# Layer two's block products over pairs of 512-token blocks, and output matmuls taken from a queue

## The chip, the core and the metric

The kernel runs on one core of one Trainium2 chip. The metric is device time in microseconds (us) of one execution, the median of several runs. Engines are called PE (matmuls) with PEld (its weight loads), DVE (vector), ACT (scalar) and SP, whose queue issues every DMA of this kernel. A PE matmul here has a 128x128 stationary operand and a moving operand of 512 or 256 columns. All values are 32 bit.

## What is computed

An attention stage over pooled keys and values makes x (4608 tokens x 512). Layer one and layer two follow:

```
h = x @ w_in                         # 512 x 2048
g = h * (1 / (1 + exp(-1.702 * h)))
x = g @ w_out                        # 2048 x 512
a, b = x @ w_a, x @ w_b              # 512 x 1536 each
return ((a * b) @ w_out2)            # 1536 x 512
```

Inputs are double precision, and the kernel splits every value into a high and a low part, so each product of the reference is three matmuls: high x high, high x low, low x high.

## The kernel before

The 4608 tokens stand in 9 blocks of 512. Work goes in passes. Layer one has two passes (`passes` 0 and 1, with 6 and 10 of its 16 slices of 128 hidden columns), layer two three (passes 2 to 4, with 4 of its 12 slices `f` each). A pass goes over all 9 blocks, and in a block over its slices; one (pass, block, slice) is a step. Partial sums over slices stay in PSUM within a pass and go through DRAM between passes: pass 2 writes them (tile `ys`, L513 to L518), pass 3 reads and writes, pass 4 reads and writes the output (L520 to L524).

Layer one: 12 matmuls make `h` and 12 make `acc` in a step, all of 512 columns (`mm3`, L132 to L135).

Layer two: for one slice, a and b over the 512 tokens are a 2 x 2 block matrix (two columns of the weights by two halves of 256 tokens), and seven block products replace eight (`products`, L419). Their operands are sums of blocks of x (seven tiles `xo` a block, 512 KB each, made at the end of pass 1 by `store_operands`, L480, kept in DRAM as `yd` and loaded again in each pass) and of weights (`wc`). Product number n is six matmuls of 256 columns into one of the PSUM banks X (two buffers), Y and Z (one each), L438. Three of the products are followed by a copy by ACT (L444, L446, L448), the others by a DVE operation (L450 to L459); DVE and ACT then make `chi` and `clo`, the two parts of a * b, for each token half (`parts`, L427). A bank that is accumulated on must have been read by that copy or operation before PE goes on writing it: product 6 waits for L444, 3 for L446, 7 for L448, 4 for L454.

The output matmuls (`out_rows`, L464) take `chi` and `clo` of 128 tokens as the stationary operand and the slice's rows of w_out2 (`wo`) as moving, three matmuls of 512 columns (L470, L471, L472) for one row c of four. `mixed` (L576) runs the products of one step between the output rows of the step before, in the order of `ORDER` (L574), where P is a product and O a row:

```
ORDER = ("P1", "P5", "O2", "P6", "O3", "P3", "P2", "P7", "O0", "O1", "P4")
```

PE's order is fixed by `after_last` (L404); the other engines' orders come from a scheduler at build time, and each engine runs its instructions in that order. `finish` (L507) evicts the four sums at the end of a block. SBUF tiles come from pools: `wp` (13 buffers of 8 KB a partition: weights and raw data), `xp` (11 of 4 KB: operands), `p2` (`st` with two buffers, `part`, `raw`, `v`), `gp`, `yp` (two buffers for `ys`).

Of the kernel before, what the change touches and what calls it, by code (L numbers as in the profile page):

```python
# [9 lines left out]
F32 = mybir.dt.float32  # L10
# [14 lines left out]
def tile_kernel(ctx, tc, q, k, v, w_in, w_out, w_a, w_b, w_o2, out):  # L25
# [30 lines left out]
    HALF = N // 2  # L56

    const = ctx.enter_context(tc.tile_pool(name="const", bufs=1))
    wp = ctx.enter_context(tc.tile_pool(name="wp", bufs=13))
    xp = ctx.enter_context(tc.tile_pool(name="xp", bufs=11))  # L60
# [82 lines left out]
    yd = [dram.tile([P, 7, 2, 2, HALF], F32, name=f"yd{j}") for j in range(NB)]  # L143
# [7 lines left out]
    def x_tiles():  # L151

        return [[xp.tile([P, 2, N], F32R, tag="x", name=nm) for _ in range(2)] for nm in ("xhi", "xlo")]
# [4 lines left out]
    def load_x(i, j):  # L158
        if passes[i][0] == 1:
            x_t[i, j] = x_tiles()  # L160
            for e in range(2):
                for h in range(2):
                    nc.sync.dma_start(out=f32(x_t[i, j][e][h]), in_=xd[j][:, e, 2 * h:2 * h + 2])
            return
        x_t[i, j] = [None] * 7
        for o in USED:
            x_t[i, j][o] = xp.tile([P, 2, 2, HALF], F32R, tag="x", name="xo")
            nc.sync.dma_start(out=f32(x_t[i, j][o]), in_=yd[j][:, o])
# [250 lines left out]
    def products(i, j, f):  # L419

        banks = {nm: ps2.tile([P, HALF], F32, tag=nm, name=nm, bufs=2 if nm == "X" else 1) for nm in "XYZ"}
        X, Y, Z = (banks[nm] for nm in "XYZ")
        s = p2.tile([P, 3, HALF], F32, tag="st", name="s")
        chi, clo = (gp.tile([P, 2, HALF], F32R, tag=tag, name=nm) for tag, nm in (("ghi", "chi"), ("glo", "clo")))
        g_t[i, j, f] = (chi, clo)

        def parts(col, src):  # L427
            nc.scalar.copy(out=chi[:, col], in_=src)  # L428
            nc.vector.tensor_tensor(out=clo[:, col], in0=src, in1=f32(chi[:, col]), op=ALU.subtract)  # L429

        def product(n):
            c, o, nm = PRODUCTS[n]
            w, at_ = w2_t[f, c]
            x = x_t[i, j][o]
            for kk in range(2):
                ks = slice(kk * P, (kk + 1) * P)
                for m, (we, xe) in enumerate(((0, 0), (0, 1), (1, 0))):
# [4 lines left out]
                    ))  # L442
            if n == 1:
                nc.scalar.copy(out=s[:, 0], in_=X)  # L444
            elif n == 5:
                nc.scalar.copy(out=s[:, 1], in_=Y)  # L446
            elif n == 6:
                nc.scalar.copy(out=s[:, 2], in_=X)  # L448
            elif n == 3:
                nc.vector.tensor_tensor(out=s[:, 2], in0=s[:, 2], in1=Y, op=ALU.add)  # L450
            elif n == 2:
                nc.vector.tensor_tensor(out=s[:, 0], in0=s[:, 0], in1=Z, op=ALU.add)
            elif n == 7:
                nc.vector.tensor_tensor(out=s[:, 1], in0=s[:, 1], in1=X, op=ALU.add)  # L454
                made = nc.vector.tensor_tensor(out=s[:, 1], in0=s[:, 1], in1=s[:, 2], op=ALU.mult)  # L455
                anchors[i, j, f] = made.ins
                parts(1, s[:, 1])
            else:
                nc.vector.tensor_tensor(out=s[:, 0], in0=s[:, 0], in1=X, op=ALU.mult)  # L459
                parts(0, s[:, 0])  # L460

        return product

    def out_rows(f, cs_, oa, c, first, last):  # L464

        chi, clo = (t[:, c // 2] for t in cs_)
        w = w_t[3, f // 2]
        whi, wlo = w[:, f % 2, :], w[:, 2 + f % 2, :]
        ts = slice(c % 2 * P, (c % 2 + 1) * P)
        after_last(nc.tensor.matmul(out=oa[c], lhsT=chi[:, ts], rhs=whi, start=first, stop=False))  # L470
        after_last(nc.tensor.matmul(out=oa[c], lhsT=chi[:, ts], rhs=wlo, start=False, stop=False))  # L471
# [35 lines left out]
    def finish(i, j, sums):  # L507
# [17 lines left out]
        if i == 1:  # L525
            store_operands(j, part_t[i, j])
# [340 lines left out]
```

## Time and profile before

| | us |
|---|---|
| median of three runs (1835.01 to 1837.60) | 1836.38 |
| profiled execution, its own time | 1838.84 |
| span of its instructions | 1837.1 |
| PE busy in the span | 1777.5 |
| DVE busy | 1092.1 |
| ACT busy | 641.2 |

The profiled execution's time is its span and 1.74 us around it. It is 2.46 us (0.13%) above the median. Attention lies mixed with pass 0 up to about 450 us, pass 1 runs to about 964 us, and layer two's three passes take the rest.

How to read the rows: start and length in us from the span's start; then the engine, the line of the kernel, the operation, the tiles as out<-in, the shape and how many alike follow each other (x6). In brackets stands idle time of the engine just before, and what ended it. A PE matmul's shown length has its drain in it, so successive matmuls overlap; what one costs is the distance of starts.

### The profile page before, as it was taken

To read this page: it belongs to the slowest core of one execution; us is meant where nothing else is said; L and a number is where in the kernel's file an instruction comes from. 1 tells how busy PE (TensorE), PEld (TensorE's weight loads), DVE (VectorE), ACT (ScalarE), POOL (GpSimd) and SP (SyncE) were. 2 spreads that over 40 slices of the span, in tenths; PEclk is the share of its full clock that TensorE was granted. 3 is DMA by queue.
4 is the path that set the end of the run, shared out by engine and by line. 5 is a ranking of instruction groups with operands and counts; after the bars stand their busy time and mean duration, and the time that the engine had idled before them with its cause. 6 is when DMAs were issued, how large, how long until landed. Compare 5 with 4: busy or idle time off the path is not lost.

```text
span 1837.1 us, 27304 instructions
## 1 busy us (share of the span) xinstructions
PE 1777.5 (97%) x10536; PEld 1548.8 (84%) x10536; DVE 1092.1 (59%) x2157; ACT 641.2 (35%) x1754; POOL 1.7 (0%) x8
## 2 busy tenths in 40 slices
PE   5789999999999999999997999998999999999999
PEld 4667888888888888888886999998999999999998
DVE  6885666655986677677535665663444444444444
ACT  5645655553332333333332323332222222222222
POOL 0000000000000000000000000000000000000000
PEclk7889999999999999999998999999999999999999
DMA  8364444335545546555683656479454548464642
GB/s 296 106 204 148 145 157 154 105 98 184 195 154 184 224 177 247 212 200 186 237 293 144 252 198 250 175 279 360 173 206 161 208 160 320 157 221 149 221 158 104
DMA packets 100546, 358.31 MB, mean 195 GB/s; under 512 B 11232, under 2 KB 11232, under 8 KB 92064
## 3 DMA queue, kind: packets, MB, share of 16 engines
q1 hardware_dynamic: 100416, 356.56, 54.2%
q8 instruction: 83, 1.36, 0.3%
q14 instruction: 47, 0.39, 0.1%
HBM read 238.55 MB, written 117.96 MB: 194 GB/s over the span
## 4 chain that ended last, share of the span: by engine, by line
PE 89%; DVE 5%; DMA 4%; ACT 2%; issue 0%; ACTq 0%; DVEq 0%; SPq 0%
PE X L438 16%; PE Y L438 8%; PE h L133 7%; PE acc L133 7%; PE h L134 7%; PE acc L134 7%; PE h L135 7%; PE acc L135 7%; PE acc L470 5%; PE acc L471 5%; PE acc L472 5%; PE Z L438 4%; PE px L284 2%; DMA part<-ys 2%; PE sc L239 2%; PE pt L271 1%
## 5 line engine op out<-in xcount | busy, mean ns | idle before, releaser
L438 PE MATMUL X<-xo,wc 128*128 128x256 f32 x2592 | 364.1, 283 | 11.5 <-ACT s L444 11.0
L438 PEld LDWEIGHTS X<-xo,wc 128*128 128x128 f32 x2592 | 348.5, 191 | 31.1 <-ACT s L444 11.8
L428 ACT CAST chi<-s 128x256 fp32r<-128x256 f32 x216 | 87.9, 407 | 439.7 <-DVE s L455 346.4
L133 PE MATMUL h<-xhi,w 128*128 128x512 f32 x576 | 227.8, 396 | 0.8 <-ACT xhi L88 0.5
L134 PE MATMUL h<-xlo,w 128*128 128x512 f32 x576 | 226.3, 393 | 0.0
L135 PE MATMUL acc<-ghi,w 128*128 128x512 f32 x576 | 225.8, 392 | 0.0
L134 PE MATMUL acc<-glo,w 128*128 128x512 f32 x576 | 225.8, 392 | 0.0
L135 PE MATMUL h<-xhi,w 128*128 128x512 f32 x576 | 225.7, 392 | 0.0
L438 PE MATMUL Y<-xo,wc 128*128 128x256 f32 x1296 | 190.2, 283 | 0.0
L385 ACT ACTIVATE g<-h 128x512 f32<-128x512 f32 x144 | 86.2, 599 | 293.7 <-PE h L135 270.7
L438 PEld LDWEIGHTS Y<-xo,wc 128*128 128x128 f32 x1296 | 178.0, 191 | 9.6
L388 DVE SCALAR_TENSOR_TENSOR g<-g,h 128x512 f32<-128x512 f32 x144 | 98.4, 684 | 142.1 <-ACT g L385 142.0
L133 PE MATMUL acc<-ghi,w 128*128 128x512 f32 x576 | 180.4, 401 | 2.3 <-ACT ghi L389 2.1
L470 PE MATMUL acc<-wo,chi 128*128 128x512 f32 x432 | 172.1, 398 | 4.8 <-ACT ys L515 4.8
L471 PE MATMUL acc<-wo,chi 128*128 128x512 f32 x432 | 171.9, 398 | 0.0
L450 DVE TENSOR_TENSOR s<-s,Y 128x256 f32<-128x256 f32 x108 | 45.5, 421 | 210.1 <-PE Y L438 208.0
L472 PE MATMUL acc<-wo,clo 128*128 128x512 f32 x432 | 169.2, 392 | 0.8 <-DVE clo L429 0.8
L429 DVE TENSOR_TENSOR clo<-s,chi 128x256 fp32r<-128x256 f32 x216 | 91.3, 424 | 85.9 <-ACT chi L428 85.9
L133 PEld LDWEIGHTS h<-xhi,w 128*128 128x128 f32 x576 | 109.5, 190 | 24.8 <-ACT aT L272 0.9
L135 PEld LDWEIGHTS h<-xhi,w 128*128 128x128 f32 x576 | 109.2, 190 | 23.1
L134 PEld LDWEIGHTS h<-xlo,w 128*128 128x128 f32 x576 | 109.3, 190 | 22.8 <-DVE raw L125 0.4
L133 PEld LDWEIGHTS acc<-ghi,w 128*128 128x128 f32 x576 | 107.1, 190 | 24.0 <-ACT ghi L389 2.9
(75 smaller groups left out, 2397.9 us busy)
## 6 DMA issues: line engine op xcount, KB each, us to landing
xo<-yd SPq DMA_DIRECT2D x189, 512.0 KB
yd<-st SPq DMA_DIRECT2D x63, 512.0 KB
part<-part SPq DMA_DIRECT2D x27, 1024.0 KB
part<-ys SPq DMA_DIRECT2D x72, 256.0 KB
raw<-in_moe_w_out_dram SPq DMA_DIRECT2D x28, 512.0 KB
wd<-ws SPq DMA_DIRECT2D x12, 1024.0 KB
wc<-wd SPq DMA_DIRECT2D x12, 1024.0 KB
xd<-xhi SPq DMA_DIRECT2D x18, 512.0 KB
```

The lines of the kernel that those rows point to most:

```text
L133: nc.tensor.matmul(out=o, lhsT=whi, rhs=xhi, start=first, stop=False)
L134: nc.tensor.matmul(out=o, lhsT=whi, rhs=xlo, start=False, stop=False)
L135: nc.tensor.matmul(out=o, lhsT=wlo, rhs=xhi, start=False, stop=last)
L385: nc.scalar.activation(out=g, in_=hps, func=AF.Tanh, scale=0.5 * 1.702)
L388: made = vec(nc.vector.scalar_tensor_tensor(out=g, in0=g, scalar=1.0, in1=hps, op0=ALU.add, op1=ALU.mult))
L428: nc.scalar.copy(out=chi[:, col], in_=src)
L429: nc.vector.tensor_tensor(out=clo[:, col], in0=src, in1=f32(chi[:, col]), op=ALU.subtract)
L438: after_last(nc.tensor.matmul(out=banks[nm], lhsT=w[:, at_, we, ks], rhs=x[:, xe, kk, :], start=n in FIRST and kk == 0 and m == 0, stop=kk ...
L450: nc.vector.tensor_tensor(out=s[:, 2], in0=s[:, 2], in1=Y, op=ALU.add)
L470: after_last(nc.tensor.matmul(out=oa[c], lhsT=chi[:, ts], rhs=whi, start=first, stop=False))
L471: after_last(nc.tensor.matmul(out=oa[c], lhsT=chi[:, ts], rhs=wlo, start=False, stop=False))
L472: after_last(nc.tensor.matmul(out=oa[c], lhsT=clo[:, ts], rhs=whi, start=False, stop=last))
```

## The change

It groups the blocks in layer two into units: blocks (1,2), (3,4), (5,6), (7,8) are four pairs, block 0 stands alone. Pass 1 now goes over the blocks 1 to 8 and then 0. In a pair the "two halves of tokens" of the 2 x 2 scheme are its two blocks, so each matmul of a product has 512 columns where it had 256, and there are half as many; operands of a pair are 1 MB each. Block 0 keeps 256 columns.

Output rows are no longer bound to the next step. Each row group (three matmuls) goes into a list `groups`, and `pop(n)` inside a step's table runs the n oldest. The second token column's rows (4 in a pair, 2 in block 0) are queued after each slice; those of the first column (`held[0, f]`, tiles `hi` and `lo`, five buffers) wait in SBUF until the unit's last slice and are then queued row by row over all four slices. A sum is evicted as its last group runs (`evict`). All big SBUF tiles, operands, weights, partial sums of layer one and (in layer two) raw weights, share one pool `wp` of 19 buffers. The last block's operand stores take their staging tiles from `wp`.

```diff
-    wp = ctx.enter_context(tc.tile_pool(name="wp", bufs=13))
-    xp = ctx.enter_context(tc.tile_pool(name="xp", bufs=11))
+    units = [(j, j + 1) for j in range(1, NB, 2)] + [(0,)]
+    NU2 = len(units)
+    order = [list(range(NB)), [j for u in units for j in u]] + [list(range(NU2))] * (L2 - L1)
+    wp = ctx.enter_context(tc.tile_pool(name="wp", bufs=19))
...
+    def load_operand(i, u, n):
+        o = USED[n]
+        if len(units[u]) == 2:
+            t = wp.tile([P, 2, 2, N], F32R, tag="w", name="xo")
...
+        nc.sync.dma_start(out=f32(t), in_=yd[u][:, o])
...
+    def out_rows(i, f, col, ti, j, c, first, last):
...
+        if first:
+            accs[i, j, c] = acc.tile([P, N], F32, tag="acc", name="acc")
+        oa = accs[i, j, c]
+        after_last(nc.tensor.matmul(out=oa, lhsT=chi[:, ts], rhs=whi, start=first, stop=False))
+        after_last(nc.tensor.matmul(out=oa, lhsT=chi[:, ts], rhs=wlo, start=False, stop=False))
+        after_last(nc.tensor.matmul(out=oa, lhsT=clo[:, ts], rhs=whi, start=False, stop=last))
+        if last:
+            evict(i, j, c, accs.pop((i, j, c)))
+
+    def pop(n):
+        for g in groups[:n]:
+            g()
+        del groups[:n]
...
-    def products(i, j, f):
-        banks = {nm: ps2.tile([P, HALF], F32, tag=nm, name=nm, bufs=2 if nm == "X" else 1) for nm in "XYZ"}
+    def products(i, u, f, table):
+        n_ = N if pair else HALF
+        banks = {nm: ps2.tile([P, n_], F32, tag=nm, name=nm, bufs=2 if nm == "X" else 1) for nm in "XYZ"}
...
+        for what in table:
+            if what[0] == "P":
+                product(int(what[1]))
+            else:
+                pop(int(what[1]))
+        groups.extend(g for _, g in rows_of(1, f, held.pop((1, f))))
+        if last:
+            per_f = [list(rows_of(0, f_, held.pop((0, f_)))) for f_ in fs]
+            for ti in range(n_ // P):
+                groups.extend(p[ti][1] for p in per_f)
...
+    def evict(i, j, c, a):
+        to = part[2][j][:, c, :] if i in WRITES else out[j * N + c * P:j * N + (c + 1) * P, :]
+        if i in READS:
+            t = part_t.pop((i, j, c))
+            nc.vector.tensor_tensor(out=t, in0=a, in1=t, op=ALU.add)
+        else:
+            t = yp.tile([P, N], F32, tag="y", name="ys")
...
+        nc.sync.dma_start(out=to, in_=t)
...
+            st = p2.tile([P, 2, 2, w_], F32R, tag="st", name="st", bufs=2)
+        else:
+            st = wp.tile([P, 2, 2, w_], F32R, tag="w", name="st")
...
-    ORDER = ("P1", "P5", "O2", "P6", "O3", "P3", "P2", "P7", "O0", "O1", "P4")
+    FIRST_F = ("O2", "P1", "O2", "P5", "O2", "P6", "O2", "P3", "O2", "P2", "O1", "P7", "O3", "P4")
+    OTHER_F = ("P1", "P5", "O1", "P6", "O1", "P3", "P2", "O1", "P7", "O3", "P4")
...
+            before.setdefault((i - 1, NU2 - 1, passes[i - 1][1][0]), []).extend(loads(i))
...
+                before.setdefault((i, u, fs[2]), []).extend(operands(i, u + 1))
```

The digit after O is now a number of groups to pop. The next unit's operands are asked for from the third step of a unit, a pass's weights and first operands from the first step of block 0 in the pass before.

**PE, a step within a pass.** Before, from products 4 and 1 (which run into each other) on; L438 is a product's matmul, L470 to L472 one output row:

```order
L438 MATMUL X<-xo,wc 128x256 x12
L438 MATMUL Y<-xo,wc 128x256 x6
L470 MATMUL acc<-wo,chi 128x512
L471 MATMUL acc<-wo,chi 128x512
L472 MATMUL acc<-wo,clo 128x512
L438 MATMUL X<-xo,wc 128x256 x6
L470 MATMUL acc<-wo,chi 128x512
L471 MATMUL acc<-wo,chi 128x512
L472 MATMUL acc<-wo,clo 128x512
L438 MATMUL Y<-xo,wc 128x256 x6
L438 MATMUL Z<-xo,wc 128x256 x6
```

The same place in the changed kernel, in a pair (L492 is a product's matmul, L445 to L447 one group of the list):

```order
L492 MATMUL X<-xo,wc 128x512 x12
L492 MATMUL Y<-xo,wc 128x512 x6
L445 MATMUL acc<-wo,ghi 128x512
L446 MATMUL acc<-wo,ghi 128x512
L447 MATMUL acc<-wo,glo 128x512
L492 MATMUL X<-xo,wc 128x512 x6
L445 MATMUL acc<-wo,ghi 128x512
L446 MATMUL acc<-wo,ghi 128x512
L447 MATMUL acc<-wo,glo 128x512
L492 MATMUL Y<-xo,wc 128x512 x6
L492 MATMUL Z<-xo,wc 128x512 x6
```

The sequence is the same, the matmuls are twice as wide, and one such step now stands for two blocks.

**PE, from the last step of a pass (block 0) to the next pass.** Before, this place reads as within a pass; from product 3 of a step to product 1 of the next:

```order
L438 MATMUL Y<-xo,wc 128x256 x6
L438 MATMUL Z<-xo,wc 128x256 x6
L438 MATMUL X<-xo,wc 128x256 x6
L470 MATMUL acc<-wo,chi 128x512
L471 MATMUL acc<-wo,chi 128x512
L472 MATMUL acc<-wo,clo 128x512
L470 MATMUL acc<-wo,chi 128x512
L471 MATMUL acc<-wo,chi 128x512
L472 MATMUL acc<-wo,clo 128x512
L438 MATMUL X<-xo,wc 128x256 x12
```

Now, at the end of pass 2:

```order
L492 MATMUL Y<-xo_9578,wc 128x256 x6
L492 MATMUL Z<-xo_9581,wc 128x256 x6
L492 MATMUL X<-xo_9581,wc 128x256 x6
L492 MATMUL X<-xo_9584,wc 128x256 x6
L445 MATMUL acc<-wo,ghi 128x512
L446 MATMUL acc<-wo,ghi 128x512
L447 MATMUL acc<-wo,glo 128x512
L445 MATMUL acc<-wo,ghi 128x512
L446 MATMUL acc<-wo,ghi 128x512
L447 MATMUL acc<-wo,glo 128x512
L492 MATMUL X<-xo,wc 128x512 x6
```

The list has run empty here: products 3, 2, 7 and 4 follow each other with no group between them, and the first groups after product 4 are those of the `ghi` that product 7 has just started.

**ACT, from layer one to layer two.** `st` is the staging tile of the last block's operand stores (L88 before, L92 after). Before:

```order
L444 COPY s<-X 128x256
L446 COPY s<-Y 128x256
L88 CAST st<-part 128x512
L448 COPY s<-X 128x256
L428 CAST chi<-s 128x256
L88 CAST st<-part 128x512
L428 CAST chi<-s 128x256
L88 CAST st<-part 128x512 x5
L444 COPY s<-X 128x256
```

Now:

```order
L500 COPY s<-X 128x512
L502 COPY s<-Y 128x512
L92 CAST st<-part 128x512 x2
L504 COPY s<-X 128x512
L477 CAST ghi<-s 128x512
L92 CAST st<-part 128x512
L477 CAST hi<-s 128x512
L500 COPY s<-X 128x512
L92 CAST st<-part 128x512
L502 COPY s<-Y 128x512
```

Five stagings stood together ahead of the second step's first copy; now the seven stand singly or in pairs between the copies.

## Rows read from the trace of the kernel before

**Rows 1.** Page: engines' busy time, and PE, its granted clock in 40 slices.

```profile
PE 1777.5 (97%) x10536; PEld 1548.8 (84%) x10536; DVE 1092.1 (59%) x2157; ACT 641.2 (35%) x1754; POOL 1.7 (0%) x8
...
PE   5789999999999999999997999998999999999999
...
PEclk7889999999999999999998999999999999999999
```

**Rows 2.** Stages: PE, PEld, DVE, ACT, POOL busy (instructions), clock, DMA share, GB/s.

```profile
500.00:950.00 450.00, 450.00 (x1987) 372.61 (x1986) 308.53 (x530) 151.01 (x244) 0.00 (x0) 1.00 0.57 208
1300.00:1800.00 500.00, 500.00 (x3469) 466.93 (x3468) 228.29 (x515) 118.13 (x322) 0.00 (x0) 1.00 0.54 196
```

**Rows 3.** Timeline, PE, one step of pass 3 (from product 4 on).

```profile
1400.73 1.59 PE L438 MATMUL X<-xo,wc 128*128 128x256 f32 x12
1402.16 0.88 PE L438 MATMUL Y<-xo,wc 128*128 128x256 f32 x6
1402.88 0.40 PE L470 MATMUL acc<-wo,chi 128*128 128x512 f32 x1
...
1403.58 0.87 PE L438 MATMUL X<-xo,wc 128*128 128x256 f32 x6
...
1408.52 1.59 PE L438 MATMUL X<-xo,wc 128*128 128x256 f32 x12
```

**Rows 4.** Groups by shape: DVE and ACT on 256 and on 512 columns.

```profile
L385 ACT ACTIVATE g<-h 128x512 f32<-128x512 f32 x144 | 86.2, 599 | 293.7 <-PE h L135 270.7 <-DVE glo L393 19.4 <-DVE raw L644 3.5
...
L521 DVE SCALAR_TENSOR_TENSOR part<-acc,part 128x512 f32<-128x512 f32 x108 | 70.7, 686 | 29.8 <-PE acc L472 21.4 <-DMA xo<-yd 4.9 <-PE acc L135 3.5
...
L454 DVE TENSOR_TENSOR s<-s,X 128x256 f32<-128x256 f32 x108 | 45.5, 421 | 30.5 <-PE X L438 30.5
```

**Rows 5.** Timeline, DVE, after product 7 of the last steps.

```profile
1828.17 0.42 DVE L454 TENSOR_TENSOR s<-s,X 128x256 f32<-128x256 f32 x1 [0.30 <-PE X L438]
1828.63 0.42 DVE L455 TENSOR_TENSOR s<-s 128x256 f32<-128x256 f32 x1
1829.53 0.43 DVE L429 TENSOR_TENSOR clo<-s,chi 128x256 fp32r<-128x256 f32 x1 [0.47 <-ACT chi L428]
```

**Rows 6.** Timeline, from layer one to layer two, several engines.

```profile
981.45 0.62 ACT L88 CAST st<-part 128x512 fp32r<-128x512 f32 x1 [1.68 <-DMA yd<-st]
...
986.24 1.65 PE L438 MATMUL X<-xo,wc 128*128 128x256 f32 x6 [10.98 <-ACT s L444]
...
988.96 1.48 PE L438 MATMUL Y<-xo,wc 128*128 128x256 f32 x6
990.24 1.37 PE L438 MATMUL Z<-xo,wc 128*128 128x256 f32 x6
```

**Rows 7.** Waits of PE: what for, us in total, times, longest.

```profile
PE pt L271 <- DVE at L263: 19.2, 6, 5.6
...
PE acc L470 <- ACT ys L515: 4.8, 2, 4.1
PE acc L472 <- DVE clo L429: 0.8, 3, 0.4
```

**Rows 8.** Timeline, PE and ACT, around the end of pass 2.

```profile
1279.59 0.60 ACT L515 ACTIVATE ys<-acc 128x512 f32<-128x512 f32 x1 [2.06 <-DMA part<-ys]
...
1280.24 0.80 PE L470 MATMUL acc<-wo,chi 128*128 128x512 f32 x1 [4.07 <-ACT ys L515]
...
1282.97 2.46 PE L438 MATMUL X<-xo,wc 128*128 128x256 f32 x12
1285.26 0.88 PE L438 MATMUL Y<-xo,wc 128*128 128x256 f32 x6
```

**Rows 9.** Stages of 10 us there, columns as in rows 2.

```profile
1230.00:1240.00 10.00, 10.00 (x72) 9.40 (x71) 4.80 (x11) 3.52 (x9) 0.00 (x0) 1.00 1.01 391
...
1280.00:1290.00 10.00, 9.76 (x53) 8.93 (x54) 2.25 (x5) 1.71 (x5) 0.00 (x0) 0.76 0.20 76
```

**Rows 10.** Waits of SP's queue, 960 to 1300 us, longest first.

```profile
SPq L168 <- PE X L438: 104.2, 36, 18.0
```

More of the change, by code (lines that the diff above doesn't have):

```diff
@@ L158, in load_x, with operands @@
     def load_x(i, j):
[L159 to L168, printed above, removed]
+        x_t[i, j] = x_tiles()
+        for e in range(2):
+            for h in range(2):
+                nc.sync.dma_start(out=f32(x_t[i, j][e][h]), in_=xd[j][:, e, 2 * h:2 * h + 2])
+    def load_operand(i, u, n):
[3 more added lines that the diff above has]
+        else:
+            if n % 2 == 0:
+                x_t[i, u, "both"] = wp.tile([P, 2, 2, 2, HALF], F32R, tag="w", name="xo2")
+            t = x_t[i, u, "both"][:, n % 2]
+        x_t[i, u, o] = t
+        nc.sync.dma_start(out=f32(t), in_=yd[u][:, o])
+    def operands(i, u):
+        return [op(load_operand, i, u, n) for n in range(7)]
     at = ExitStack()
@@ L417, in tile_kernel @@
     FIRST, LAST = (1, 2, 5), (2, 3, 4)
[L419 to L429 removed]
+    groups = []
@@ new lines, in pop, with st, col_tiles, rows_of @@
+    def pop(n):
+        for g in groups[:n]:
+            g()
+        del groups[:n]
+    held = {}
+    def products(i, u, f, table):
+        fs = passes[i][1]
+        pair = len(units[u]) == 2
+        n_ = N if pair else HALF
+        first, last = f == fs[0], f == fs[-1]
+        banks = {nm: ps2.tile([P, n_], F32, tag=nm, name=nm, bufs=2 if nm == "X" else 1) for nm in "XYZ"}
+        X, Y, Z = (banks[nm] for nm in "XYZ")
+        s = {}
+        def st(n):
+            s[n] = p2.tile([P, n_], F32, tag="st", name="s", bufs=4)
+            return s[n]
+        def col_tiles(pool, bufs, *tags):
+            return tuple(pool.tile([P, n_], F32R, tag=tag, name=tag, bufs=bufs) for tag in tags)
+        def parts(col, src):
+            chi, clo = col
+            nc.scalar.copy(out=chi, in_=src)
+            nc.vector.tensor_tensor(out=clo, in0=src, in1=f32(chi), op=ALU.subtract)
+        def rows_of(col_n, f, col):
+            for ti in range(n_ // P):
+                j, c = (units[u][col_n], ti) if pair else (units[u][0], 2 * col_n + ti)
+                yield c, op(out_rows, i, f, col, ti, j, c, f == fs[0], f == fs[-1])
@@ L462, in products @@
[L462 to L471, printed above, removed]
-        after_last(nc.tensor.matmul(out=oa[c], lhsT=clo[:, ts], rhs=whi, start=False, stop=last))
@@ new lines, in products, with load_part, load_rows @@
+        groups.extend(g for _, g in rows_of(1, f, held.pop((1, f))))
+        if last:
+            per_f = [list(rows_of(0, f_, held.pop((0, f_)))) for f_ in fs]
+            for ti in range(n_ // P):
+                groups.extend(p[ti][1] for p in per_f)
+    part_t = {}
+    def load_part(j):
+        part_t[j] = wp.tile([P, KD, N], F32, tag="w", name="part")
+        nc.sync.dma_start(out=part_t[j], in_=part[1][j])
+    def load_rows(i, u, col):
+        for ti in range(4 if len(units[u]) == 2 else 2):
+            j, c = (units[u][col], ti) if len(units[u]) == 2 else (units[u][0], 2 * col + ti)
+            if col == 0 and ti < 2:
+                t = yp.tile([P, N], F32, tag="y", name="part")
+            else:
+                t = p2.tile([P, N], F32, tag="part", name="part", bufs=4)
+            part_t[i, j, c] = t
+            nc.sync.dma_start(out=t, in_=part[2][j][:, c, :])
@@ L507, in finish @@
     def finish(i, j, sums):
-        layer = passes[i][0]
-        half = 0.5 if layer == 1 else 1.0
-        for c in (2, 3, 0, 1) if layer == 2 else range(4):
+        for c in range(4):
             if i not in READS:
@@ L819, in tile_kernel @@
             second(s)
+    pop(len(groups))
 def _laid_out(name, a):
```

230 lines of the change are left out of this document (141 added, 89 removed).

## The prediction

> **What bounds the kernel now.** I read the page first. PE is busy 97% of the span, DVE 59%, ACT 35%, and in the slices PE is at 9 nearly everywhere from the fifth on, with PEclk at 9 [rows 1]. So the time is a stream of matmuls plus the few places where the stream breaks, and a change is worth what it does to the distance between matmul starts, and to the breaks. Both have to be read from stages.
>
> The stages come next [rows 2]. From 500 to 950 us (pass 1) every matmul has 512 columns: 1987 in 450 us, 226.5 ns each, at a granted clock of 1.00, which is 2.4 GHz. From 1300 to 1800 us (layer two) 3469 matmuls of both widths fill 500 us without a gap, also at 1.00. Neither stage waits for DVE, ACT or DMA (DMA share 0.57 and 0.54).
>
> The timeline of one layer-two step splits the mix [rows 3]. The twelve matmuls of products 4 and 1 take 1400.73 to 1402.16, 1.43 us or 119.2 ns each for 256 columns. One output row, three matmuls of 512, takes 1402.88 to 1403.58, 0.70 us or 233.3 ns each. 42 x 119.2 + 12 x 233.3 ns is 7.81 us, and the step takes 7.79 (1400.73 to 1408.52). So a matmul costs its columns at 2.4 GHz (106.7 and 213.3 ns) and some 12.5 ns more for 256, 13.2 for 512 in layer one, 20 for 512 in output rows. That extra is paid per matmul, and it is what wider matmuls save.
>
> Then the breaks. Between the layers PE stands 10.98 us, because ACT's copy L444 is queued behind stagings that each wait for a store to land, 1.68 us at a time; after it PE runs at the lower level, 4.00 us (986.24 to 990.24) for twelve matmuls of 256 and an output row that cost 1.43 + 0.70 at full clock [rows 6]. Together 12.9 us. At the end of pass 2 PE waits 4.07 us for an eviction that waited for the store before it, with the clock at 0.76 behind it: two rows and twelve products take 1280.24 to 1285.26, 5.02 us, against 2.83 [rows 8, 9]. With the other waits of that kind (4.8 + 0.8 us in all [rows 7]) that is 7.8 us. The waits of the attention stage (19.2 us the largest) the change doesn't aim at.
>
> **The change part by part.**
>
> *Products.* Four of five units are pairs: 7 products x 6 matmuls x 12 slices x 4 pairs = 2016 matmuls of 512 columns stand for 4032 of 256; block 0 keeps its 504. All are on PE's path. The trace has no layer-two product of 512 columns; the nearest rows are layer one's 226.5 ns (weights stationary, tokens moving, as in a product) and the output rows' 233.3 ns (the other way round). I take 226.5, because the products of 256 show the same extra per matmul as layer one and not the rows' 20 ns. 2 x 119.2 - 226.5 = 11.9 ns, x 2016 = **-24.0 us**. By 233.3 it is 5.1 ns and -10.3 us. On the other side, should the output rows (still 1296 matmuls) fall to 226.5 once all around them is 512 wide, 8.8 us more go: -32.8.
>
> A page of the Trainium skill says that this width should hardly matter: "TensorE: Matmul & The Clock Gate", section "Back-to-back issue gap", gives N / 2.4 + 2.5 ns between matmuls at the full clock, 109.2 and 215.8 ns. By it the products would give 2016 x 2.5 ns, 5.0 us, and the kernel would end near 1831. The rows disagree: the extra is 12.5 and 13.2 ns here, not 2.5, so I go by the rows and keep the page as a small rival.
>
> *DVE and ACT.* A product's operation grows from 421 to 686 ns on DVE, ACT's to some 0.6 us [rows 4], and there are half as many: less work in all, off the path. Which wait ends last must be seen from the table. Product 6 waits for the copy of product 1 (0.6 us and some 0.1 for each handing over, against a product of 1.36 us and a group between them), 3 for 5 and 7 for 6 likewise; product 4 waits for the operation after 7 (0.69 + 0.2), covered by three groups, 2.1 us. Covered, so 0. The tightest cover is at a unit's start, where the first groups need the `ghi` and `glo` that product 7 of the step before began: that chain is 1.79 us for 256 columns [rows 5], at 512 about 2 x 0.69 + 0.62 + 0.69, 2.7 to 2.9, against three groups and product 4, 3.46. Also 0; with the cover gone, as below, it shows.
>
> *Empty list.* Block 0 queues half as many groups as its tables pop, so the list runs dry around each pass's start. In the first step of a pass product 4 then has nothing between it and 7: 0.9 us. In the three after it has one group, 0.70 of the 0.9: 0.2 each. That is 1.5 per pass, 4.5 for three, less the first 0.9, which lies in the next item: 3.6. At the last step of block 0 (256 columns) 0.42 + 0.2 stand open, and the first `ghi` afterwards comes about 0.1 late: 0.7, three times. **+5.7 us**, from 0 (if the waits fit into drains) to about 12 (if the hand-overs are twice as long).
>
> *Between the layers.* The seven stagings now stand between the copies, the order shows. On DVE four evictions, two `lo` parts, two subtractions and three operations of the first step stand before product 4 may start: 11 x 0.686 = 7.5 us, while PE has four products, 24 x 226.5 ns = 5.4. So 2.1 + 0.2, and I add one store's landing, 1.7, for the stagings that follow: 4.0 left of 12.9, and no fall of the clock. **-8.9 us**; from 0 (stagings block as before) to -12.9.
>
> *Pass ends.* At a pass's end the same bytes as before are loaded (weights 9 MB and operands), and DMA is full there now (share 1.01, 391 GB/s [rows 9]). Evictions come one by one instead of four together, but the four rows of a pair's second column still come within 4 us, with two `ys` buffers. I leave the 7.8 us of pass 2's end as they are and add 3 for pass 3's, where partial rows must now land one by one through the same full queue: **+3 us**, from -7.8 to +13 (one break as in rows 8, 6.3 us, twice).
>
> *Rest.* In pass 1 `wp` must hold ten weights, four tiles of x, three of partial sums and two staged weights, 19 of 19 buffers: just enough, 0. The attention stage is rescheduled by the wider pool; its waits [rows 7] can move by some us either way: 0, +-5. At the end one eviction stands where three did (-1.4), but ten groups run with nothing beside them: 0.
>
> Sum: -24.0 - 8.9 + 5.7 + 3 = -24.2 us. The rows come from an execution of 1838.84 (span 1837.1 and 1.74 around it), so its like would be 1814.6; against the median of 1836.38, which is 2.46 lower, **1812 us**.
>
> **The rivals.**
>
> 1. *Products at the rate of output rows.* 13.7 us of the gain are missing: 1826. For it: it is layer two's only 512-wide rate. Against: 256-wide products in the same stage have no such extra.
> 2. *The break between the layers stays.* If stores land late behind the new operand loads, ACT blocks as in rows 6: 1812 + 8.9 = 1821.
> 3. *Everything fits better.* Output rows at 226.5 as well and the pass ends without a break: 1812 - 8.8 - 10.8 = about 1793.
> 4. *Width is worth 2.5 ns*: 1831, as above.
> 5. *Breaks at every unit (slower).* SP issues all DMAs in order. Today it already stands 104.2 us in layer two's first third for operand buffers, once 18.0 us [rows 10], with evictions' stores queued behind. Now three operand buffers are free for the next unit's seven, the other four wait for products of the unit's last step, and right after it come the four evictions that need stored tiles back. If a store lands later than the about 5 us that the table leaves it, ACT or DVE blocks with PE behind it, for 4.07 us and a lower clock, 6.3 in all [rows 8]. There are 14 such places; four of them eat the forecast's gain (24.2 / 6.3), seven make 1812 + 44 = 1856, all 1900. Against it: the next unit's operands are due only at its products 3 to 4, some 20 us later, and between pass ends DMA is at 0.54.
>
> That the change doesn't do what it says is ruled out by the order: products stand there with 512 columns.
>
> **How the numbers follow.** The forecast has 0.47, rival 1 0.16, rival 2 0.11, rival 3 0.11, rival 4 0.03, rival 5 0.12. A measurement of this kernel can tell 0.2%, 3.7 us, from no change. All cases but the fifth end below 1832.7: 0.88, less 0.03 where bounds add up (rival 4 and 1 with a stall): faster 0.85. Same 0.06, half from there and half from rival 5 with four or five places. Slower 0.09. The range goes from rival 3, 1793, to rivals 1 and 2 together, 1812 + 13.7 + 8.9 = 1835.
>
> **What would show it.** Pair steps of layer two: 42 + 24 matmuls, 42 x 226.5 + 24 x 233.3 ns = 15.1 us from product 1 to the next product 1, against two times 7.79. A product's six starts 1.36 us apart (1.40 in rival 1). Between the layers a wait of PE for DVE's operation before product 4 of some 2 us, and PEclk unbroken. At pass starts short waits of PE for DVE at product 4, below 1 us. The prediction is wrong if PE's waits in layer two add up to more than 30 us, if the clock falls inside passes, or if pass 1 no longer fills PE.

## The result and the profile after

The changed kernel takes **1806.30 us** (median of four runs, 1805.71 to 1807.52), the kernel before 1836.89 beside it (1835.01 to 1837.60). The ratio is 0.9836, with a 95% interval of 0.9819 to 0.9853: 30.6 us or 1.6% faster. The prediction was 1812 with a range of 1793 to 1835. Direction and range hold, and the gain is some 6 us larger than the sum said. Five of its six terms were off by 4 to 9 us each, with both signs.

The profiled execution took 1807.52 us (span 1805.4). Its page, first the engines' busy time, then PE's granted clock in 40 slices:

```profile
PE 1748.8 (97%) x8520; PEld 1440.9 (80%) x8520; DVE 1043.2 (58%) x1821; ACT 606.7 (34%) x1514; POOL 1.7 (0%) x8
...
PEclk9889999999999999999999999999999999999999
```

2016 fewer matmuls, 29 us less PE, and the same share of 97% [rows 1]. The 9 of the clock is no longer broken in the second half, but the slices show nothing else. The stages do:

```profile
500.00:950.00 450.00, 450.00 (x1987) 372.75 (x1986) 310.35 (x539) 151.77 (x246) 0.00 (x0) 1.00 0.54 202
1300.00:1800.00 500.00, 497.49 (x2338) 414.93 (x2337) 206.79 (x326) 99.69 (x182) 0.00 (x0) 1.00 0.53 195
```

Pass 1 is as it was, matmul for matmul (1987 in 450 us, as in [rows 2]). In layer two 2338 matmuls stand where 3469 stood, and PE now idles for 2.5 us where it idled for none. One step of a pair, PE's timeline:

```profile
1391.98 2.88 PE L492 MATMUL X<-xo,wc 128*128 128x512 f32 x12
1394.70 1.52 PE L492 MATMUL Y<-xo,wc 128*128 128x512 f32 x6
1396.06 0.39 PE L445 MATMUL acc<-wo,ghi 128*128 128x512 f32 x1
...
1396.74 1.52 PE L492 MATMUL X<-xo,wc 128*128 128x512 f32 x6
...
1405.58 2.88 PE L492 MATMUL X<-xo,wc 128*128 128x512 f32 x12
```

A product's six starts are 1.36 us apart (1394.70 to 1396.06), 226.7 ns a matmul. An output row takes 1396.06 to 1396.74, **0.68 us**, where it took 0.70 [rows 3]. The step has 42 + 18 matmuls in 13.60 us, again 226.7 each: the two kinds of matmul now cost the same.

Where PE waits, from 950 us on (what for, us in total, times, longest). A wait is counted only from the end of the drain of the matmul before it, so a stop costs somewhat more than is listed:

```profile
PE X L492 <- DVE s L510: 4.9, 8, 0.8
PE acc L445 <- ACT ys L557: 3.1, 1, 3.1
PE acc L447 <- DVE glo L478: 0.6, 3, 0.2
```

The wait of 10.98 us between the layers [rows 6] is gone; ACT's `ys` costs 3.1 where it cost 4.8 [rows 7]; the first line, product 4 behind the operation after product 7, was one wait of 0.5 us before. Between the layers the timeline, PE first, then DVE and ACT:

```profile
970.06 1.52 PE L492 MATMUL X<-xo,wc 128*128 128x512 f32 x6
...
975.50 1.52 PE L492 MATMUL X<-xo,wc 128*128 128x512 f32 x6
...
979.58 1.52 PE L492 MATMUL X<-xo,wc 128*128 128x512 f32 x6
981.89 3.01 PE L492 MATMUL X<-xo,wc 128*128 128x512 f32 x12 [0.78 <-DVE s L510]
984.74 1.52 PE L492 MATMUL Y<-xo,wc 128*128 128x512 f32 x6
...
974.34 2.48 DVE L610 SCALAR_TENSOR_TENSOR part<-acc,part 128x512 f32<-128x512 f32 x4 [4.10 <-PE acc L139]
...
981.14 0.69 DVE L510 TENSOR_TENSOR s<-s,X 128x512 f32<-128x512 f32 x1 [0.59 <-PE X L492]
...
985.10 0.58 ACT L500 COPY s<-X 128x512 f32<-128x512 f32 x1
...
988.01 0.62 ACT L92 CAST st<-part 128x512 fp32r<-128x512 f32 x1 [1.12 <-DMA yd<-st]
988.53 0.58 ACT L504 COPY s<-X 128x512 f32<-128x512 f32 x1
991.03 0.62 ACT L92 CAST st<-part 128x512 fp32r<-128x512 f32 x1 [1.91 <-DMA yd<-st]
```

The stagings (L92) still wait for stores to land, 1.12 and 1.91 us, but copies that PE needs (L500, L504) stand between them. One wait of 0.78 us is left. DVE had done all that stands ahead of L510 before product 7 ended (it idled 0.59 us for PE), so the 0.78 is only what product 4 always waits if nothing lies between it and product 7. Behind it the twelve matmuls take 2.85 us (981.89 to 984.74), against 2.72 in the pair's step above.

The first product starts at 970.06 us, 5.7 later than the 964.39 of the kernel before, and the last matmul at 1801.22 instead of 1832.85. So layer two went from 868.5 to 831.2 us, 37.3 less, and attention with layer one gave 5.7 of it back. What follows the last matmul is the same (4.2 and 4.3 us to the end of the span).

### The profile page after: what moved, and what is told of

The parts are those of the page before. It is cut to its first block, busy times and chain, and to the rows that moved or that the text cites. A ratio compares the mean times of both kernels' runs of the same rounds, so it can differ in the third digit from the quotient of the medians.

```text
span 1805.4 us, 22434 instructions
## 1 busy us (share of the span) xinstructions
PE 1748.8 (97%) x8520; PEld 1440.9 (80%) x8520; DVE 1043.2 (58%) x1821; ACT 606.7 (34%) x1514; POOL 1.7 (0%) x8
## 4 chain that ended last, share of the span: by engine, by line
PE 90%; DVE 5%; DMA 3%; ACT 1%; issue 0%; SPq 0%; ACTq 0%; DVEq 0%
PE X L492 16%; PE Y L492 8%; PE h L137 7%; PE h L138 7%; PE h L139 7%; PE acc L138 7%; PE acc L137 7%; PE acc L139 7%; PE acc L447 5%; PE acc L445 5%; PE acc L446 5%; PE Z L492 4%; PE px L298 2%; PE sc L253 2%; PE pt L285 1%; DVE vs L238 1%
## 5 line engine op out<-in xcount | busy, mean ns | idle before, releaser
L492 PE MATMUL X<-xo,wc 128*128 128x512 f32 (+1 forms) x1440 | 329.5, 369 | 5.7 <-DVE s L510 4.9
L492 PEld LDWEIGHTS X<-xo,wc 128*128 128x128 f32 x1440 | 254.3, 188 | 59.4 <-DVE s L510 12.6
L138 PE MATMUL acc<-glo,w 128*128 128x512 f32 x576 | 226.5, 393 | 4.2 <-DVE glo L407 4.2
L137 PE MATMUL h<-x,w 128*128 128x512 f32 x576 | 228.0, 397 | 2.3 <-DVE g L402 1.6
L138 PE MATMUL h<-x,w 128*128 128x512 f32 x576 | 226.4, 393 | 0.0
L139 PE MATMUL h<-x,w 128*128 128x512 f32 x576 | 226.2, 393 | 0.0
L492 PE MATMUL Y<-xo,wc 128*128 128x512 f32 (+1 forms) x720 | 167.2, 368 | 0.0
L492 PEld LDWEIGHTS Y<-xo,wc 128*128 128x128 f32 x720 | 128.0, 188 | 23.7
L137 PEld LDWEIGHTS h<-x,w 128*128 128x128 f32 x576 | 109.6, 190 | 26.7 <-DVE g L402 2.2
L138 PEld LDWEIGHTS acc<-glo,w 128*128 128x128 f32 x576 | 108.8, 189 | 27.0 <-DVE glo L407 4.6
L139 PEld LDWEIGHTS h<-x,w 128*128 128x128 f32 x576 | 109.3, 190 | 23.1
L138 PEld LDWEIGHTS h<-x,w 128*128 128x128 f32 x576 | 109.4, 190 | 22.8 <-DVE raw L129 0.4
L403 ACT CAST ghi<-g 128x512 fp32r<-128x512 f32 x144 | 90.0, 625 | 110.9 <-DVE g L402 74.4
L139 PEld LDWEIGHTS acc<-ghi,w 128*128 128x128 f32 x576 | 108.7, 189 | 22.6 <-issue 0.4
L137 PEld LDWEIGHTS acc<-ghi,w 128*128 128x128 f32 x576 | 106.9, 189 | 23.3 <-ACT ghi L403 2.5
L407 DVE TENSOR_TENSOR glo<-g,ghi 128x512 fp32r<-128x512 f32 x144 | 98.9, 687 | 36.1 <-ACT ghi L403 35.1
```

Of the source, the lines that this page charges most:

```text
L137: nc.tensor.matmul(out=o, lhsT=whi, rhs=xhi, start=first, stop=False)
L138: nc.tensor.matmul(out=o, lhsT=whi, rhs=xlo, start=False, stop=False)
L139: nc.tensor.matmul(out=o, lhsT=wlo, rhs=xhi, start=False, stop=last)
L403: nc.scalar.copy(out=ghi, in_=g)
L407: return rest, lambda: vec(nc.vector.tensor_tensor(out=glo, in0=g, in1=f32(ghi), op=ALU.subtract))
L492: after_last(nc.tensor.matmul(out=banks[nm], lhsT=w[:, at_, we, ks], rhs=x[:, xe, kk, :], start=n in FIRST and kk == 0 and m == 0, stop=kk ...
```

## Experiments

Times are medians, each beside runs of the kernel before on the same chip (1836.8, 1837.4 and 1837.6 us in the three series).

**1. Single blocks: what is the width worth?** All else of the change stays (the list, the held products, the shared pool), but every unit is one block of 256-column products. The tables take half as many groups, the other blocks' staging tiles come from a pool that has room, and weight preparation is spread over two units where it was over one pair.

```diff
-    units = [(j, j + 1) for j in range(1, NB, 2)] + [(0,)]
+    units = [(j,) for j in range(1, NB)] + [(0,)]
...
-    FIRST_F = ("O2", "P1", "O2", "P5", "O2", "P6", "O2", "P3", "O2", "P2", "O1", "P7", "O3", "P4")
-    OTHER_F = ("P1", "P5", "O1", "P6", "O1", "P3", "P2", "O1", "P7", "O3", "P4")
+    FIRST_F = ("O1", "P1", "O1", "P5", "O1", "P6", "O1", "P3", "O1", "P2", "P7", "O2", "P4")
+    OTHER_F = ("P1", "P5", "O1", "P6", "P3", "P2", "P7", "O2", "P4")
```

> The list of output groups, the holding of the first column, the one pool and the order of blocks stay as in the changed kernel; only the pairs are undone (nine units of one block, 256 columns a product, tables that pop half as many groups). Theory (width is the gain): products return to 119 ns a matmul and output rows, again between narrow products, from 226.5 to some 232 ns: 4536 x 119.2 + 1296 x 232.3 ns = 842 us of matmuls in layer two against 812 in the changed kernel, so 1806 + 30 = 1836 us, within 6. Rival (list, pool and order are the gain, width only a few us): 1806 to 1815. In both, an output row's three matmuls tell whether wide matmuls are slower next to narrow ones: 0.70 us if they are, 0.68 if they are not.

Measured: 1830.80 us (1830.13 to 1832.29), ratio 0.9969 (0.9957 to 0.9981). The width is worth 24.5 us of the 30.6, and list, order and pool together 6. That lies at the lower edge of what was expected (1836, within 6). By the rates below, products (23.6) and output rows (6.1) are 29.7 us; layer two of the profiled execution, first product to last matmul, is 26.9 longer (966.76 to 1824.78, 858.0 us against 831.2), so single blocks stop PE for some 3 us less, and the rest lies ahead of layer two. One row and one product of its timeline (PE):

```profile
1403.72 0.40 PE L445 MATMUL acc<-wo,ghi 128*128 128x512 f32 x1
...
1404.42 0.40 PE L445 MATMUL acc<-wo,ghi 128*128 128x512 f32 x1
...
1406.54 0.88 PE L492 MATMUL Y<-xo,wc 128*128 128x256 f32 x6
1407.26 0.40 PE L445 MATMUL acc<-wo,ghi 128*128 128x512 f32 x1
```

The row is back at 0.70 us (1403.72 to 1404.42), though it comes from the same list and the same code as in the changed kernel. So an output row costs 0.70 beside products of 256 columns and 0.68 beside products of 512. The rows' extra is not a property of the rows.

**2. The kernel before with one pool: what did layer one lose?** Only the pool: 19 buffers shared, two operands (or two x tiles) to a buffer.

```diff
-    wp = ctx.enter_context(tc.tile_pool(name="wp", bufs=13))
-    xp = ctx.enter_context(tc.tile_pool(name="xp", bufs=11))
+    wp = ctx.enter_context(tc.tile_pool(name="wp", bufs=19))
...
-        for o in USED:
-            x_t[i, j][o] = xp.tile([P, 2, 2, HALF], F32R, tag="x", name="xo")
+        for n, o in enumerate(USED):
+            if n % 2 == 0:
+                both = wp.tile([P, 2, 2, 2, HALF], F32R, tag="w", name="xo2")
+            x_t[i, j][o] = both[:, n % 2]
```

> The kernel before with one change: operands and x tiles come from one pool of 19 buffers instead of two pools of 13 and 11. In the changed kernel layer two starts 5.7 us later than before (970.1 against 964.4). Theory (the pool reorders the loads of the attention stage): here too the first product starts near 970, PE is busy some 38 us between 100 and 150 us instead of 43.8, and the time is 1837 + 6 = 1843 us if layer two is not touched by the pool. Rival (the loss comes from something else in the change, as the order of blocks in pass 1): first product at 964.4, 1837 us.

Measured: 1852.05 us (1847.65 to 1854.89), ratio 1.0080 (1.0065 to 1.0095). Slower by 15, more than expected. The profiled execution (1847.65) is the fastest of the four; it is 8.8 above the kernel before's, and 7.1 of that lies in layer two (875.5 us against 868.5). Its waits of PE there:

```profile
PE X L440 <- ACT s L446: 11.9, 1, 11.9
PE acc L472 <- ACT ys L517: 8.5, 3, 4.3
```

The break between the layers is there (11.9), so the pool did not cure it, and the waits for `ys` grow (4.8 before). For layer one the run speaks through its order: the sequence on DVE in the attention stage is the changed kernel's, instruction for instruction, up to 489 us. There `glo` of an early step has moved behind key and value sums and weight preparation. DVE of the changed kernel at that place, and below it PE:

```profile
118.63 1.35 DVE L226 TENSOR_REDUCE ks<-kraw 128x144 f32<-128x1152 f32 x1 [1.17 <-DMA kraw<-in_k_dram]
...
121.20 0.68 DVE L402 SCALAR_TENSOR_TENSOR g<-g,h 128x512 f32<-128x512 f32 x1
...
127.49 0.68 DVE L134 TENSOR_TENSOR w<-tmp,raw 128x512 fp32r<-128x512 f32 x1
128.09 0.68 DVE L407 TENSOR_TENSOR glo<-g,ghi 128x512 fp32r<-128x512 f32 x1
...
128.83 0.79 PE L138 MATMUL acc<-glo,w 128*128 128x512 f32 x1 [4.17 <-DVE glo L407]
```

A key sum that waits for its DMA stands ahead of `g`, and `glo` comes 6.9 us after `g` (121.20 to 128.09). In the kernel before that sum was behind both, and `glo` came 3.2 us after (115.09 to 118.32). The first product of this run starts at 966.07, less late than expected, and between 100 and 150 us PE is busy for 41.5 us, where 38 were expected (43.8 before, 38.2 in the changed kernel): the order came over, its whole price in this one execution did not. How much of that is chance is seen from eight profiled executions whose program is the changed kernel's in the attention stage (its own and seven of experiments 1 and 3 to 8): 966.8 to 970.1, 968.3 on average. So layer one lost about 3.9 us against the one profiled execution of the kernel before (964.39), and the 5.7 of the profile is the upper end.

**3. Product 2 as the cover of product 4.** At a pass's start the list runs dry, and product 4 has nothing between it and product 7. Product 2, which needs neither, is moved there.

```diff
-... "O2", "P3", "O2", "P2", "O1", "P7", "O3", "P4")
+... "O2", "P3", "O2", "P7", "O1", "P2", "O3", "P4")
-    OTHER_F = ("P1", "P5", "O1", "P6", "O1", "P3", "P2", "O1", "P7", "O3", "P4")
+    OTHER_F = ("P1", "P5", "O1", "P6", "O1", "P3", "P7", "O1", "P2", "O3", "P4")
```

> The changed kernel with product 2 moved between products 7 and 4 in both tables; the same groups are popped. Where the list is empty, product 2 (1.36 us) now covers the 0.9 us of DVE's operation after product 7. Theory (the empty list costs PE about 0.9 us at pass starts and 0.2 to 0.7 in other steps): PE's waits for L510 (4.9 us in the trace, and drains beside them) go, 1806 - 5 = 1801 us, between 1798 and 1804. Rival (those waits are hidden in drains or taken back later): 1806 within 1.5.

Measured: **1798.38 us** (1796.62 to 1798.74), ratio 0.9788 (0.9774 to 0.9801): 7.9 less than the changed kernel. The waits of PE that are left from 950 us on:

```profile
PE acc L445 <- ACT ys L557: 2.9, 1, 2.9
PE X L492 <- DMA xo<-yd: 2.0, 1, 2.0
PE acc L447 <- DVE glo L478: 0.6, 3, 0.2
```

The waits for L510 are gone, all eight. From 1250 to 1300 us, a pass's start, PE is busy for 50.00 us where it was for 48.92, so the empty list is what they were. The wait of 2.0 us for an operand is new, and the clock falls behind it and behind the wait for `ys` (3.9 and 4.8 us in all for these two stops). So layer two is only 5.9 us shorter than in the changed kernel's profile (825.2 against 831.2), and the rest of what the two executions differ by lies ahead of it, where their programs are the same.

**4. One staging tile.** The last block's stagings share one buffer, so that each must wait for the one before to land.

```diff
-            st = wp.tile([P, 2, 2, w_], F32R, tag="w", name="st")
+            st = p2.tile([P, 2, 2, w_], F32R, tag="st1", name="st", bufs=1)
```

> The changed kernel with the last block's seven operand stagings on a single buffer of their own instead of buffers of the large pool, so each staging must wait for the store before it to land. Theory (the break between the layers went because the stagings stand singly between the copies of a step that is twice as long): PE's wait there stays below 4 us, 1806 to 1810 us. Rival (it went because there are buffers for the stagings): the stagings serialise, six landings of 2 us or more stand before the copies of the second step, PE waits about 10 us and its clock falls, 1816 to 1820 us.

Measured: 1815.37 us (1814.84 to 1817.18), ratio 0.9884 (0.9871 to 0.9898), 9.1 more, outside both expected ranges. But the place it was meant for is nearly as before: PE waits 0.78 us there and 0.45 once more in the third step, though ACT's stagings now wait up to 3.43 us each. Most of the loss is 50 us on, where the scheduler, with other buffers, put other work in front. ACT, then PE:

```profile
1042.12 0.62 ACT L477 CAST ghi<-s 128x512 fp32r<-128x512 f32 x1 [11.27 <-DVE s L511]
1042.64 0.58 ACT L557 COPY ys<-acc 128x512 f32<-128x512 f32 x1
...
1043.28 0.79 PE L445 MATMUL acc<-wo,hi 128*128 128x512 f32 x1 [4.89 <-ACT ys L557]
```

The copy `ys`, which frees a bank of `acc`, stands behind a `ghi` that waits for DVE, and DVE does weight slices first; PE waits 4.89 us and then runs slowly (0.79 us for a matmul that is shown with 0.39; granted clock 0.50 from 1043 to 1046 us). So this run tells less than it should about the landings. Two more were made for that.

**5 and 6. The old order with the new tiles.** In the kernel before, five of the seven stagings stood in a row ahead of ACT's copy for step two. The changed kernel gets that order back (the copy behind the last of the seven), by a dependency without a semaphore, once with its shared tiles and once with one staging buffer.

```diff
-        nc.scalar.copy(out=hi, in_=src)
+        casts.append(nc.scalar.copy(out=hi, in_=src).ins)
...
-                nc.scalar.copy(out=st(0), in_=X)
+                made = nc.scalar.copy(out=st(0), in_=X)
+                if (i, u, f) == (L1, 0, fs[1]):
+                    tc.add_manual_dep(
+                        made.ins, casts[-1].name,
...
```

> The changed kernel, but ACT's copy of step two's first product (layer two) is ordered behind all seven stagings of the last block, as in the kernel before; the staging tiles still come from the shared pool. Theory A (the break of 11 us was the landing of stores, because two staging buffers stood behind an in-order ACT): with free buffers the stagings run on at 0.6 to 0.7 us each, PE waits 2 to 4 us at step two's copy, time 1808 to 1811. Theory B (standing behind the stagings is what costs, however fast they land): a wait of 8 to 11 us with a low clock behind it, time 1815 to 1819.

> The same order as in the run with the copies behind the stagings, and only one staging buffer for the last block. Theory A: each of six stagings waits for a landing of 1.7 to 3.4 us, the break of the kernel before is back or longer, 10 to 20 us: time 1816 to 1826, and at least 7 us above the run with free buffers. Theory B: within 3 us of that run. With this one buffer but the products' copies between the stagings the time was 1815.4, with no break at this place.

Measured: 1815.75 us (1814.51 to 1817.38), ratio 0.9880 (0.9865 to 0.9895), and 1827.60 us (1827.05 to 1829.52), ratio 0.9950 (0.9937 to 0.9962). The order with shared tiles, ACT and PE:

```profile
986.30 0.62 ACT L94 CAST st<-part 128x512 fp32r<-128x512 f32 x1 [2.13 <-DMA yd<-st]
988.23 0.62 ACT L94 CAST st<-part 128x512 fp32r<-128x512 f32 x1 [1.31 <-DMA yd<-st]
990.39 0.62 ACT L94 CAST st<-part 128x512 fp32r<-128x512 f32 x1 [1.55 <-DMA yd<-st]
990.92 0.58 ACT L502 COPY s<-X 128x512 f32<-128x512 f32 x1
...
991.55 2.93 PE L494 MATMUL X<-xo,wc 128*128 128x512 f32 x6 [6.15 <-ACT s L502]
```

The same with one buffer:

```profile
987.36 0.62 ACT L94 CAST st<-part 128x512 fp32r<-128x512 f32 x1 [3.51 <-DMA yd<-st]
...
1003.61 0.62 ACT L94 CAST st<-part 128x512 fp32r<-128x512 f32 x1 [3.43 <-DMA yd<-st]
1004.14 0.58 ACT L502 COPY s<-X 128x512 f32<-128x512 f32 x1
...
1004.77 2.93 PE L494 MATMUL X<-xo,wc 128*128 128x512 f32 x6 [19.69 <-ACT s L502]
```

With the old order the break is back: 6.15 us, the lower clock behind it (2.93 us for a product that is shown with 1.52; granted clock 0.50 from 991 to 995 us), and 2.72 more for product 4 in the step after, 9.5 us in all. Theory A was wrong that the shared pool has free buffers: three of the stagings still wait 1.3 to 2.1 us each. It was right that landings set the size: with one buffer each costs 3.4 to 3.5 us, and the break is 19.7 (the time is 1.6 us above its range). Theory B has the time of the first run right, though the wait is below its 8 to 11 us, and fails on the second, which is 11.9 us slower with the same queue. Together: whether there is a break is a matter of **order** (with the copies in between, one buffer makes none), and how long it is, of the landings that stand in front.

**7. Four buffers for `ys`.** The two added ones lie in the pool of layer two.

```diff
-            t = yp.tile([P, N], F32, tag="y", name="ys")
+            t = p2.tile([P, N], F32, tag="ys", name="ys", bufs=2) if c % 2 else yp.tile([P, N], F32, tag="y", name="ys")
```

> The changed kernel with four buffers in place of two for evicted rows of pass 2 (ys). Theory: the wait of 3.07 us at the end of pass 2 (an output row for ACT's ys, which waits for a store to land) and the low clock behind it go: 3 to 5 us less, 1801.5 to 1803.5. Rival (DMA is full there, and the same wait moves to the partial rows, the operands or the weights): 1805 to 1808.

Measured: 1801.43 us (1800.58 to 1804.67), ratio 0.9807 (0.9794 to 0.9821), 4.9 less. In the changed kernel the end of pass 2 looks like this (ACT, then PE):

```profile
1217.54 0.58 ACT L557 COPY ys<-acc 128x512 f32<-128x512 f32 x1 [1.78 <-DMA part<-ys]
...
1218.18 0.50 PE L445 MATMUL acc<-wo,hi 128*128 128x512 f32 x1 [3.07 <-ACT ys L557]
```

With four buffers PE's wait for `ys` is in its list no more, and from 1200 to 1250 us PE is busy for 49.29 us where it was for 46.22, with DMA no emptier (share 0.97 and 0.92). So it was the buffer, not the DMA traffic. In the profiles layer two is 4.2 us shorter (826.9 against 831.2).

**8. Both.** The edits of 3 and 7 together.

> Product 2 as the cover of product 4 (1798.4 alone) and four ys buffers together. If the ys wait goes and the gains add up: 1793.5 to 1795.5. If the ys wait is replaced by another one: 1797 to 1799.

Measured: 1793.02 us (1792.39 to 1793.63), ratio 0.9758 (0.9745 to 0.9772), 13.3 less than the changed kernel, where 7.9 and 4.9 make 12.8. In layer two's profiles it is 13.5 (817.7 against 831.2). Two kinds of wait of PE are left after 950 us, 0.8 us for an operand and 0.6 in all for `glo`.

**9 and 10. The order in layer one's first steps.** On top of both, DVE is asked for `glo` before other filling work: one piece earlier, or directly after `g` and before three pieces.

```diff
         in_order(hs[n][0])
-        filler(1)
         in_order(hs[n][1])
-        filler(1)
+        filler(2)
```

> The kernel with product 2 as cover and four ys buffers (1793.0), and in the first steps of layer one DVE's glo of a step is asked for ahead of the second of four pieces of weight preparation, not behind it. Theory (layer one lost 2.4 to 5.7 us because the shared pool moved glo behind key and value sums and weight preparation on DVE, with PE waiting 4.2 us for it): that wait goes, layer two's first product starts at 964 to 967, time 1788 to 1791. Rival (the attention stage is bound by its own chain, PE then waits elsewhere): first product at 967 to 970, time 1792 to 1795.

> The same base, but g and glo both stand behind one piece of weight preparation and ahead of three. Theory: as in the run with glo ahead of the second piece, 1788 to 1791, and the weights, which now come later, hide behind PE. Rival: the weights come late, PE waits for them in place of glo: 1793 to 1800.

Measured: **1788.76 us** (1787.11 to 1790.65), ratio 0.9736 (0.9722 to 0.9749), and 1794.06 us (1793.14 to 1796.47), ratio 0.9768 (0.9755 to 0.9782). From the waits of PE in the whole run, of the faster and then of the other:

```profile
PE acc L138 <- DVE glo L407: 1.0, 2, 0.8
...
PE pt L285 <- DVE g L402: 4.1, 1, 4.1
```

The wait for `glo` fell from 4.2 us to 1.0, and layer two's first product starts at 966.06, 2.8 earlier than in the run of experiment 8 (968.90), whose layer two is as long. With three pieces behind it, the wait for `glo` is gone too, but one of 4.1 us for `g` comes in its place and the gain is lost. Most of what layer one lost was the order on DVE, and that much can be had back. The 1788.76 us are the best of this study, 17.5 less than the changed kernel.

## Why the prediction was right, and where its sum was not

Its terms are taken against the profiled executions: layer two lost 37.3 us, and layer one took 5.7. A stop is counted here by the distance between the starts of two matmuls, less what such a matmul costs in the stream (119.2 ns for 256 columns; for 512, 226.7, and 232.0 in output rows of the kernel before).

| term | predicted | shown |
|---|---|---|
| products of 512 columns | -24.0 | -23.6 |
| output rows | 0 (rival 3: -8.8) | -6.1 |
| break between the layers | -8.9 | -13.2 |
| empty list | +5.7 | +11.4 |
| pass ends, with other small stops | +3 | -5.9 |
| attention and layer one | 0, +-5 | +5.7 (3.9 on average) |

**Products: right.** 2 x 119.2 - 226.7 = 11.7 ns, times 2016 is 23.6. The choice of layer one's rate over that of the output rows was the important one, and rival 1 (1826) fell with it. So did rival 4. By the page "TensorE: Matmul & The Clock Gate" of the Trainium skill, section "Back-to-back issue gap", whose formula is given there for an isolated gap, 512 columns would start every 215.8 ns and the width would be worth 2.5 ns each. The trace has 226.7 and 11.7, and single blocks cost 24.5 us.

**Output rows: the step that failed most plainly.** "I take 226.5, because the products of 256 show the same extra per matmul as layer one and not the rows' 20 ns" treated the 20 ns as belonging to the rows, and put what they might gain into rival 3 alone. It belongs to their neighbours: in the old step of 7.79 us, 42 x 119.2 ns leave 232.0 for each of 12 row matmuls, now they take 226.7, and 1152 of them stand in pairs: 5.3 x 1152 = 6.1 us. Experiment 1 shows the link. There the rows' own tiles are narrower too (`ghi` and `hi` have 256 columns), but that is not it: the changed kernel's last rows are block 0's, with tiles of 256 columns and no product near, and fifteen starts lie 3.17 us apart, 226.4 ns each:

```profile
1798.05 0.39 PE L445 MATMUL acc<-wo,hi 128*128 128x512 f32 x1
...
1801.22 0.39 PE L447 MATMUL acc<-wo,lo 128*128 128x512 f32 x1
```

**Between the layers: right in mechanism, the remainder mis-sized.** By starts 14.3 us were there (the 12.9 leave out product 4's wait of 0.54 us in the first step and what was slow after 990.24), and 1.1 is left, not 4.0. "11 x 0.686 = 7.5 us" of DVE against 5.4 of PE was to leave 2.1. But DVE's operations start about 0.61 us apart there, not 0.686 (the four evictions take 2.48), and the evictions began at 974.34, 1.2 us before layer one's last matmul was through (product 1 of the second step starts at 975.50): they come one by one as the sums end. DVE was ready first. The 1.7 us for one landing fell behind the copies. Why the break went is shown by experiments 4 to 6: the order, as the prediction had read from it.

**Empty list: right in kind, sized at half.** The waits for L510 are listed with 4.9 us, but they cost more. In a pass's first step product 7 to product 4 takes 2.31 us (979.58 to 981.89) instead of 1.36, and the twelve matmuls after it 2.85 instead of 2.72: 1.1, where "0.9 us" was said. The three steps behind lose 0.4 to 1.0 each, where it said "0.2 each". Block 0's last step was given 0.7:

```profile
1242.40 0.88 PE L492 MATMUL X<-xo,wc 128*128 128x256 f32 x6
1243.80 0.98 PE L492 MATMUL X<-xo,wc 128*128 128x256 f32 x6 [0.51 <-DVE s L510]
1244.69 0.50 PE L445 MATMUL acc<-wo,ghi 128*128 128x512 f32 x1
...
1245.96 0.39 PE L445 MATMUL acc<-wo,ghi 128*128 128x512 f32 x1
```

Product 7 to product 4 takes 1.40 us instead of 0.72, product 4 itself 0.89, and the row behind it, which waits for `glo`, 1.27 instead of 0.68: 1.4, three times. In all it is 11.4 us without the first 1.1, near the upper end of the range that was given (about 12). Experiment 3, which removes the waits for L510 by another edit, shows the cause; in its trace 0.7 us of each of block 0's last steps is left.

**Pass ends: wrong in sign.** "I leave the 7.8 us ... and add 3 for pass 3's." At pass 3's end nothing is lost: PE's list has no wait for a partial row. At pass 2's end the one wait of 3.07 us remains, 3.4 by starts, and other small stops of layer two (2.2 us by starts before) are down to 0.6. That it is the two `ys` buffers was said there; that a fuller DMA queue would add to it was not borne out. Part of it is chance: in this execution the granted clock stayed at 1.00 behind the wait (1200 to 1250 us), while in the profiled executions of experiments 3 to 6 the same wait of 2.9 to 3.0 us has the lower clock behind it and costs 4.7 to 4.8. The 4.9 of experiment 7, a difference of medians, is nearer to those.

**Layer one: the unknown.** It had a bound and no value, and the value came out at its edge, 5.7 in the profile and 3.9 on average. The order of the changed kernel could have shown it: a key sum ahead of `g` and `glo` is there to be read. The prediction looked at the order between the layers only.

**Steps.** "42 + 24 matmuls ... 15.1 us" for a pair's step was 42 + 18 and 13.60: a step takes six rows from the list, and the rest follow at the next unit's first step. The sum is not touched by it.

**Rival 5**, breaks at every unit, did not come: SP's queue does stand for long (`SPq L179 <- PE X L492` 64.3 us in 12 waits, 21.7 the longest, against 104.2, 36 and 18.0 in [rows 10]), but no wait of PE for an operand is in the changed kernel's list. In experiment 3 there is one, of 2.0 us.

The total beat the forecast by a sum of misses with both signs: rows (6.1), the break (4.3) and the pass ends (8.9) gave 19.3 us more than said; layer one (5.7), the list (5.7) and the products (0.4) took 11.8 back. That makes 7.5; between the profiled executions it is 7.1 (1814.6 against 1807.52), between the medians 5.7. That the products carry the gain was foreseen; that the sum came within 6 us is in part luck.

## What to carry to other kernels

- A queue that is served in order turns a slow store into a stop of PE only if what PE needs stands behind it. Put the copies for the next step between the stores' stagings; more buffers shorten the stop, order removes it.
- When a list of filling work can run dry, look for work in the step itself that has no dependence on the late result and move it there. One swap in a table was worth 7.9 us here by the medians (5.9 in the profiles' layer two), where the whole rewrite gave 30.6.
- A shared pool changes what a scheduler does far away. Compare the order of every engine in every stage, not only where the change was meant.

## What the runs showed of the hardware

- A matmul of 512 columns costs 226.7 ns among others of 512, and a row of three costs 0.70 us instead of 0.68 when its neighbours are products of 256. Mixed widths cost about 5 ns on the wide ones; why was not tried. Rows of block 0 with no product near them are at 226.4 ns again.
- With one staging buffer, ACT waits 3.4 to 3.5 us between two stagings of 0.62 us each (experiment 6). The wait holds DVE's 0.69 us for the low part and the landing of a 512 KB store.
- Behind the same wait of PE, 2.9 to 3.1 us at the end of pass 2, the granted clock stayed at 1.00 in one profiled execution and fell in four others, where the stop cost 4.7 to 4.8 us instead of 3.4.
- The same program reaches layer two between 966.8 and 970.1 us in eight profiled executions. Differences of a few us in one profiled execution are not yet an effect.
